# Moving one Relu and half of one scaling from ScalarE to VectorE in a sparse-attention and expert-routing kernel

## The chip, the core and the metric

The kernel runs on one core of a Trainium2 chip. The metric is the device time of one execution in microseconds (us). The engines are written as the profile writes them: PE is TensorE (matmuls), PEld its weight loads, ACT is ScalarE, DVE is VectorE, POOL is GpSimd and SP is SyncE. Each runs its own list of instructions in the order of the program and waits on semaphores that the other engines count up.

## The reference

Two layers stand behind each other. The first is an attention that selects chunks of 32 keys by an upper bound on their scores; the second sends each token to one of eight experts.

```python
def _attn_ref(q, k, v):                       # (4, 8, 768, 64) each
    k_min, k_max = min and max of k over each chunk of 32 keys
    ub = np.sum(np.maximum(q * k_min, q * k_max), axis=-1)     # a bound per query and chunk
    top_chunks = np.argsort(where(causal, ub, -1e9))[..., -6:]
    scores = where(selected and causal, q @ k.T / 8, -1e9)
    return softmax(scores) @ v

def _moe_ref(x, w_gate, w1, w2):              # x: (3072, 512), 8 experts, hidden size 1024
    expert_idx = np.argmax(x @ w_gate, axis=1); gate_w = its softmax probability
    for e in range(8):
        ye = np.maximum(x[expert_idx == e] @ w1[e], 0.0) @ w2[e]
        out[expert_idx == e] = gate_w[...] * ye
```

## The kernel before, in words

**Attention.** The 32 pairs of batch and head are worked off two heads at a time, in 16 steps called pairs (0 to 15). For a pair, `kt` and `qt` turn k and q on PE into PSUM tiles `pk` and `pq` (two banks each, from a pool of three buffers). From `pk`, DVE makes the maximum of each chunk (`kr0`) and its negated minimum (`kr1`) into the tile `KK`, and ACT makes a bfloat16 copy (`kc`). From `pq`, ACT makes three things: the positive part of q (`qR`), the positive part of -q (`qN`) and a bfloat16 copy (`qc`). The bound of the reference is then two products that PE adds up in the PSUM tile `pc` (`ub`): positive part of q with the maxima, positive part of -q with the negated minima. From `pc`, DVE finds the sixth-best chunk of each query (`sel1`, `selb`, `sel2a`, `sel2b`, `sel3`, `selt`) and makes the mask tile `mt`, which PE adds to the scores (`sc0` to `sc5`). ACT takes exponentials (`ex`), POOL cuts the causal diagonal (`cm`), PE multiplies with v (`av`), DVE adds up denominators (`ac`).

**Experts.** The tokens' rows are scattered to memory in expert order, and 26 tiles of 128 rows (j = 0 to 25) are read back. For each tile PE makes the hidden layer (`U`), ACT its Relu (`Rl`), a transposing DMA turns it (`H`), PE multiplies with w2 into the PSUM tile `py` of one bank (`D`), ACT scales the 512 columns by the row's gate weight into `y` (`Y`, the function `down_act`), and POOL issues an indirect DMA that writes the rows of `y` to the output (`O`). After the last tile every engine loads a count `late_i` and branches over a block for rare extra tiles.

**Order.** The order of the work is a list written out by hand, `ORDER`: each word is a step and its pair or tile, and each step issues its instructions on its engines at that place in the list. A tile framework adds the semaphore waits. Steps `z.n` are n matmuls on a zeroed tile without a use for the result, which fill TensorE's idle time at the start. ACT's list begins with the load of its function table; the framework puts it ahead of the first activation.

The change touches `qe` (which makes `qR` and `qN`), `down_act`, and one line of `ORDER`.

Of the kernel before, what the change touches and what calls it, by code (L numbers as in the profile page):

```python
# [9 lines left out]
FP32 = mybir.dt.float32  # L10
BF16 = mybir.dt.bfloat16
I32 = mybir.dt.int32
AF = mybir.ActivationFunctionType
ALU = mybir.AluOpType
# [8 lines left out]
def kernel(  # L23
# [10 lines left out]
    nc = tc.nc  # L34

    B, H, S, D = q.shape
# [5 lines left out]
    DM = H * D  # L42
# [12 lines left out]
    NS = NA + NL + ND + NF2  # L55
# [4 lines left out]
    Q0 = S - NQB * 64  # L60
# [162 lines left out]
    def qe(i, nm):  # L223
        s = st[i]
        s[nm] = work.tile([128, NQB, 2, 32], FP32, tag=nm, name=nm)
        nc.scalar.activation(s[nm][:].rearrange("p j c w -> p (j c w)"), s["pq"][:, Q0:S], AF.Relu,  # L226
                             scale=1.0 if nm == "qR" else -1.0)

    def qc(i):
        nc.scalar.activation(KQ[i % 2][:, 1], st[i]["pq"], AF.Copy)  # L230
# [287 lines left out]
    tag_all = const.tile([128, JT, 2], I32)  # L518
# [167 lines left out]
    fs = [dict() for _ in range(NTILE)]  # L686
# [3 lines left out]
    def kind(j):  # L690
        if j < NA + NL:
            return "whole", j
        if j < NA + NL + ND:
            return "mixed", NFULL + NF2 + j - NA - NL
        if j < NS:
            return "first", NFULL + j - NA - NL - ND
        if j < NS + NB - NL:
            return "whole", NA + NL + j - NS
        return "second", NFULL + NF2 + ND + j - NS - NB + NL
# [113 lines left out]
    def down_act(j):  # L813
        tag, pool, bufs = (("v", ld, LDB["v"]), ("ot", work, 2))[j % 2]
        y = pool.tile([128, DM], FP32, tag=tag, bufs=bufs, name="y")
        nc.scalar.activation(y[:], fs[j]["py"][:], AF.Copy, bias=0.0, scale=tag_all[:, kind(j)[1], 0:1].bitcast(FP32))  # L816
        fs[j]["y"] = y

    def put(j):
# [25 lines left out]
    def sm_c(i):  # L845
# [3 lines left out]
    rb_ = lambda f, *a: (lambda i: f(i // HP, *a))  # L849
    fn = dict(lk=sg(load, "k"), lq=sg(load, "q"), lv=sg(load, "v"), w=load_w,  # L850
              kt=kt, kr0=sg(kred, 0), kr1=sg(kred, 1), kc=kc, qt=qt, qR=sg(qe, "qR"), qN=sg(qe, "qN"), qc=qc, ub=ub_c,
              sel1=sel1, selb=selb, sel2a=sg(sel2, 0, 5), sel2b=sg(sel2, 5, NQB), sel3=sel3, selt=selt,
              ocB=sg(oc, 0), ocA=sg(oc, 1), sm=sm_c, gt=gt, uc=uc, ut=ut, rcp=rcp, lgt=lgt, lga=lga, xt=xt, xr=xr,
              ra=rb_(r_add), rb=rb_(r_max), rc=rb_(r_shift), rx=rb_(r_exp), rd=rb_(r_cand), re=rb_(r_first),
              rf=rb_(r_hot), rg=rb_(r_sum), rh=rb_(r_eps), ri=rb_(r_gate), rk=rb_(r_rank), rm=rb_(r_row),
              rn=rb_(r_pick), ro=rb_(r_slot), rp=rb_(r_int),
              g=gather, x=x_in, z=idle_mm, xc=x_tag, U=up_mm, Rl=up_act, H=up_turn, D=down_mm, Y=down_act, O=put, dr=lambda n: nc.gpsimd.drain(), sp=pause, wg=load_gate)
    for u in range(6):
        fn.update({f"sc{u}": sg(sc, u), f"ex{u}": sg(ex, u), f"cm{u}": sg(cm, u), f"av{u}": sg(av, u),
                   f"ac{u}": sg(ac, u), f"s{u}": rb_(r_scat, u)})  # L860

    def steps(gen, n, last):
# [7 lines left out]
    x_slots += [t_[:].rearrange("p a s -> p (a s)")[:, ds(512 * n, 512)] for t_ in (KQ[0], KQ[1]) for n in range(3)]  # L870

    ORDER = """
        lk.0 lq.0 lq.1 lk.1 lv.0 lv.1 wg.0 kt.0 z.2 qt.0 kr0.0 qN.0 qR.0 kr1.0 z.3 ub.0 kc.0 qc.0 qt.1 sel1.0 selb.0
        sel2b.0 kt.1 qR.1 sel2a.0 sel3.0 kc.1 qN.1 selt.0 qc.1 z.4 sc0.0 ex0.0 sc3.0 sc1.0 kr0.1 kr1.1 ex3.0 ex1.0
        ub.1 sel1.1 selb.1 sc2.0 ex2.0 cm3.0 lk.2 lq.2 w.19 sc4.0 av1.0 sel2b.1 sel2a.1 av2.0 kt.2 w.15 sc5.0 sel3.1
        ac2.0 selt.1 ex4.0 qt.2 qc.2 ex5.0 av3.0 qN.2 lq.3 kr0.2 cm4.0 kr1.2 ac4.0 cm0.0 ac3.0 cm5.0 av4.0 qR.2
# [71 lines left out]
    for step in ORDER.split():  # L948
        nm, n = step.split(".")
# [6 lines left out]
    with tc.If(more[0] > 0) as _:  # L956
        for j0 in range(NS, NTILE, 3):
            for j in range(j0, min(j0 + 3, NTILE)):
                gather(j)
                x_in(j)  # L960
                x_tag(j)
            for j in range(j0, min(j0 + 3, NTILE)):
                up_mm(j)
                up_act(j)
                up_turn(j)
            for j in range(j0, min(j0 + 3, NTILE)):
                down_mm(j)
                down_act(j)
                put(j)
# [35 lines left out]
```

## Time and profile before

| | |
|---|---|
| median of 3 runs | 302.18 us (299.79 to 308.25) |
| the profiled execution: its time | 299.35 us |
| its span, from the first to the last instruction | 297.5 us |
| outside the span | 1.85 us |
| PE busy | 285.5 us (96% of the span) |
| DVE busy | 197.2 us (66%) |
| ACT busy | 189.1 us (64%) |
| POOL busy | 156.9 us (53%) |

The start of the span (0 to about 13 us) is filled by loads and by the first pair's chain, the stretch up to about 202 us by attention, then up to 291.85 us by expert tiles; the last tile's output leaves after that. The time of an execution is the span and some 1.85 us around it. All rows below are of this one execution.

### The profile page before, as it was taken

How to read it: one execution, taken by the hardware profiler on the slowest of the kernel's cores; microseconds unless marked ns; L12 is line 12 of the kernel's file. 1: busy time of each engine (PE TensorE's matmuls, PEld its weight loads, DVE VectorE, ACT ScalarE, POOL GpSimd, SP SyncE). 2: the span in 40 equal slices, each digit the busy share in tenths (PEclk: the TensorE clock that was granted, in tenths of full speed). 3: DMA queues.
4: the chain of work that ended last, by engine and by line, in shares of the span. 5: the costliest groups of instructions: out<-in, count | busy, mean ns of one | idle time of the engine just before them, and what ended most of it. 6: DMA issues, size and time to landing. Idle time of an engine off the chain costs nothing.

```text
span 297.5 us, 8589 instructions
## 1 busy us (share of the span) xinstructions
PE 285.5 (96%) x3105; PEld 145.5 (49%) x3105; DVE 197.2 (66%) x613; ACT 189.1 (64%) x266; POOL 156.9 (53%) x245
## 2 busy tenths in 40 slices
PE   7899999998999999999999999999999999999992
PEld 3454554554555545555556555444444444444450
DVE  6687988989999999999999999885810312000000
ACT  1879778677777786777787877543443644444541
POOL 5064442652434657724468987431685557753543
PEclk9999999999999999999999999999999999999999
DMA  8999999898997999989999999899999999999662
GB/s 153 198 196 202 190 197 216 162 222 183 176 199 132 204 195 224 203 166 189 197 229 193 210 210 258 144 150 137 191 177 255 176 223 240 223 186 220 155 140 78
DMA packets 132587, 56.51 MB, mean 190 GB/s; under 512 B 121915, under 2 KB 121917, under 8 KB 132544
## 3 DMA queue, kind: packets, MB, share of 16 engines
q1 hardware_dynamic: 117440, 29.13, 53.9%
q0 software_dynamic: 12224, 26.78, 45.2%
q10 hardware_dynamic: 2880, 0.02, 1.7%
q8 instruction: 28, 0.46, 0.7%
q14 instruction: 15, 0.12, 0.1%
HBM read 53.26 MB, written 9.99 MB: 213 GB/s over the span
## 4 chain that ended last, share of the span: by engine, by line
PE 69%; DVE 12%; POOL 5%; issue 4%; DMA 4%; ACT 3%; SPq 1%; POOLq 0%; DVEq 0%; ACTq 0%
PE ph L783 15%; PE oa L324 14%; PE py L809 12%; DVE Pa L335 6%; PE ps L288 5%; PE pc L242 5%; PE ps L296 4%; PE pc L352 3%; DMA w_all<-in_moe_w_dram 2%; PE ob L324 2%; DVE KK L214 2%; PE pc L362 2%; PE px L199 2%; PE pq L208 2%; POOL out_dram L820 2%
## 5 line engine op out<-in xcount | busy, mean ns | idle before, releaser
L304 ACT ACTIVATE Pa<-ps 128x1024 f32<-128x1024 f32 x64 | 65.1, 1024 | 16.0 <-PE ps L296 12.6
L335 DVE TENSOR_TENSOR Pa<-Pa 128x1024 f32<-128x1024 f32 (+2 forms) x64 | 65.7, 1027 | 6.2 <-PE oa L324 1.9
L324 PE MATMUL oa<-Pa,v 128*64 128x512 f32 (+2 forms) x320 | 64.3, 518 | 0.0
L311 POOL TENSOR_SCALAR_AFFINE_SELECT Pa<-Pa 128x256 f32<-128x256 f32 x48 | 25.5, 547 | 52.0 <-ACT Pa L304 49.4
L809 PE MATMUL py<-w_all,hT 128*128 (+2 forms) x256 | 47.2, 379 | 0.0
L792 ACT ACTIVATE h<-ph 128x1024 bf16<-128x1024 f32 (+1 forms) x27 | 26.6, 991 | 26.7 <-DMA hT<-h 12.5
L288 PE MATMUL ps<-KQ 64*128 64x512 bf16 (+3 forms) x256 | 37.3, 307 | 1.1 <-ACT Pa L304 0.6
L820 POOL DMA_INDIRECT out_dram<-y,tag_all x26 | 25.6, 986 | 19.4 <-ACT y L816 14.9
L296 PE MATMUL ps<-mt,IND 64*128 64x256 bf16 (+4 forms) x512 | 34.2, 225 | 0.3 <-DVE mt L272 0.3
L500 POOL DMA_INDIRECT xs_dram<-xrow,sli x24 | 26.9, 1121 | 14.3 <-DVE cnt L527 5.6
L809 PEld LDWEIGHTS <-hT 128*128 128x128 bf16 (+1 forms) x256 | 20.8, 102 | 24.5 <-issue 1.7
L816 ACT ACTIVATE y<-py,tag_all 128x512 f32<-128x512 f32 x26 | 17.7, 686 | 21.1 <-PE py L809 17.5
L214 DVE TENSOR_REDUCE KK<-pk 128x24 f32<-128x768 f32 x32 | 29.1, 943 | 1.3 <-PE pk L208 1.3
L324 PEld LDWEIGHTS oa<-Pa,v 128*64 128x64 f32 x320 | 19.4, 136 | 19.8 <-issue 14.6
L288 PEld LDWEIGHTS <-KQ 64*128 64x128 bf16 x256 | 13.1, 93 | 28.4 <-issue 28.1
L296 PEld LDWEIGHTS <-IND 64*128 64x128 bf16 x512 | 23.1, 94 | 7.5 <-issue 0.4
L783 PE MATMUL ph<-w_all,x_early 128*128 (+1 forms) x128 | 25.5, 379 | 0.1
L182 POOL DMA_DIRECT2D w_all<-in_moe_w_dram x32 | 23.9, 747 | 0.0
L311 POOL TENSOR_SCALAR_AFFINE_SELECT Pb<-Pb 128x256 f32<-128x256 f32 x32 | 18.8, 614 | 9.5 <-ACT Pb L304 9.4
L783 PE MATMUL ph<-w_all,KQ 128*128 (+2 forms) x128 | 21.9, 380 | 0.0
L752 DVE TENSOR_TENSOR tag_all<-tag_all,inv_i 128x1 int32<-128x1 int32 x10 | 1.6, 162 | 28.0 <-DMA tag_all<-xs_dram 28.0
L226 ACT ACTIVATE qN<-pq 128x576 f32<-128x576 f32 x16 | 10.5, 653 | 14.8 <-PE pq L208 14.7
(167 smaller groups left out, 449.5 us busy)
## 6 DMA issues: line engine op xcount, KB each, us to landing
w_all<-in_moe_w_dram POOLq DMA_DIRECT2D x32, 512.0 KB, 6.6
k<-in_k_dram SPq DMA_DIRECT2D x32, 192.0 KB
q<-in_q_dram SPq DMA_DIRECT2D x32, 192.0 KB
v<-in_v_dram SPq DMA_DIRECT2D x32, 192.0 KB
hT<-h SPq DMA_TRANSPOSE x27
out_dram<-y,tag_all POOLq DMA_INDIRECT x26, 4.1
xs_dram<-xrow,sli POOLq DMA_INDIRECT x24, 6.5
tag_all<-xs_dram ACTq DMA_DIRECT2D x20, 1.0 KB
```

Source lines behind the costliest of these rows:

```text
L214: nc.vector.tensor_reduce(KK[i % 2][:, n, 0:NCH], st[i]["pk"].rearrange("p (c w) -> p c w", w=CH), AX.X, ALU.max if n == 0 else ALU.min, n ...
L288: nc.tensor.matmul(ps[:, hd, ds(c0, w)], lhsT=kc_[r, ts(kb_, 128)], rhs=qc_[r, ds(q0, w)], start=True, stop=False, skip_group_check=True)
L296: nc.tensor.matmul(o[:, :, c, :], lhsT=IND[c][r, ts(kb_, 128)], rhs=mt[r, ds(j0, n), :], start=False, stop=True, skip_group_check=True)
L304: nc.scalar.activation(P[:], st[i][f"ps{u}"][:, :, 0:w], AF.Exp)
L311: nc.gpsimd.affine_select(out=pd, in_=pd, pattern=[[0, 2], [1, 128]], compare_op=ALU.is_ge, fill=0.0, base=0, channel_multiplier=-1)
L324: nc.tensor.matmul(po[64 * hd:64 * hd + 64, ds(q0 - o0, w)], lhsT=vt[:, kb_, hd, :], rhs=P[:, hd, ds(c0, w)], start=(u <= 1 and n == 0), s ...
L335: nc.vector.tensor_tensor(a[:, :, ds(q0_, w)], a[:, :, ds(q0_, w)], P[:, :, ds(c0, w)], ALU.add)
L500: d = nc.gpsimd.indirect_dma_start(out=xs_dram[:], out_offset=bass.IndirectOffsetOnAxis(ap=sli[:, u:u + 1], axis=0), in_=bst[b]["xrow"][:, ...
L783: nc.tensor.matmul(ph[r, fh, :], lhsT=fs[j]["xT"][:, c, r], rhs=w1_all[:, ds(wo + c * F + fh * 512, 512)], start=(c == 0), stop=(c == NDC ...
L792: nc.scalar.activation(h_[:, a].rearrange("q a (c j p) -> q (a c) j p", c=2, j=2), fs[j]["ph"][:, a].rearrange("q a (c p j) -> q (a c) j p ...
L809: nc.tensor.matmul(py[r], lhsT=fs[j]["hT"][:, c, r], rhs=w2_all[:, ds(wo + c * DM, DM)], start=(c == 0), stop=(c == NFC - 1), skip_group_c ...
L820: d = nc.gpsimd.indirect_dma_start(out=out[:], out_offset=bass.IndirectOffsetOnAxis(ap=tag_all[:, kind(j)[1], 1:2], axis=0), in_=fs[j]["y" ...
```

## The change: what it does

For pair 0 alone, the positive part of -q (`qN.0`) is made by DVE, as a multiplication by -1 and a maximum with 0, in place of an ACT Relu with scale -1. In `ORDER` the step is moved from ahead of `qR.0` to behind `kr1.0`. For the last expert tile alone (j = 25), ACT scales columns 0 to 255 of `py` and DVE columns 256 to 511.

```diff
     def qe(i, nm):
         s = st[i]
         s[nm] = work.tile([128, NQB, 2, 32], FP32, tag=nm, name=nm)
-        nc.scalar.activation(s[nm][:].rearrange("p j c w -> p (j c w)"), s["pq"][:, Q0:S], AF.Relu,
-                             scale=1.0 if nm == "qR" else -1.0)
+        dst = s[nm][:].rearrange("p j c w -> p (j c w)")
+        if (i, nm) == (0, "qN"):
+            nc.vector.tensor_scalar(dst, s["pq"][:, Q0:S], -1.0, 0.0, ALU.mult, ALU.max)
+        else:
+            nc.scalar.activation(dst, s["pq"][:, Q0:S], AF.Relu, scale=1.0 if nm == "qR" else -1.0)
...
     def down_act(j):
...
-        nc.scalar.activation(y[:], fs[j]["py"][:], AF.Copy, bias=0.0, scale=tag_all[:, kind(j)[1], 0:1].bitcast(FP32))
+        gate, w = tag_all[:, kind(j)[1], 0:1].bitcast(FP32), DM // 2 if j == NS - 1 else DM
+        nc.scalar.activation(y[:, 0:w], fs[j]["py"][:, 0:w], AF.Copy, bias=0.0, scale=gate)
+        if w < DM:
+            nc.vector.tensor_scalar(y[:, w:DM], fs[j]["py"][:, w:DM], gate, None, ALU.mult)
...
     ORDER = """
-        lk.0 lq.0 lq.1 lk.1 lv.0 lv.1 wg.0 kt.0 z.2 qt.0 kr0.0 qN.0 qR.0 kr1.0 z.3 ub.0 kc.0 qc.0 qt.1 sel1.0 selb.0
+        lk.0 lq.0 lq.1 lk.1 lv.0 lv.1 wg.0 kt.0 z.2 qt.0 kr0.0 qR.0 kr1.0 qN.0 z.3 ub.0 kc.0 qc.0 qt.1 sel1.0 selb.0
```

Three places of the instruction lists follow, with the semaphores that each instruction waits for: `PE_49` counts PE's instructions, `DVE_49` VectorE's, `Activation_49` ScalarE's, `Pool_49` GpSimd's, and names with DMA count transfers. Lines behind 226 have numbers higher by 3 in the changed kernel, behind 816 by 6.

ScalarE's list from its first instruction, before:

```order
L226 ACT_TABLE_LOAD
L226 ACTIVATE qN<-pq 128x576 [waits PE_49]
L226 ACTIVATE qR<-pq 128x576 [waits DVE_49,Pool_49]
L218 ACTIVATE KQ_124<-pk 128x768 [waits DVE_49]
L230 ACTIVATE KQ_124<-pq 128x768
L226 ACTIVATE qR<-pq 128x576 [waits PE_49,Activation_49]
```

ScalarE's list at the same place now:

```order
L230 ACT_TABLE_LOAD [waits DVE_49,PE_49]
L230 ACTIVATE qR<-pq 128x576 [waits Pool_49]
L218 ACTIVATE KQ_124<-pk 128x768 [waits DVE_49]
L233 ACTIVATE KQ_124<-pq 128x768 [waits DVE_49]
L230 ACTIVATE qR<-pq 128x576 [waits PE_49,Activation_49]
```

The first activation is now `qR.0`, which has three waits, and two of them (VectorE, and PE for the last transpose of `qt.0`) stand ahead of the table load instead of behind it; the copy `qc.0` (L233) has a new wait for VectorE.

VectorE's list around the chunk reductions of pair 0, before:

```order
L167 TENSOR_SCALAR tri_164<-rev_150 128x8 x8
L214 TENSOR_REDUCE KK_126<-pk 128x24 [waits PE_49]
L214 TENSOR_REDUCE KK_126<-pk 128x24
L251 STREAM_TRANSPOSE ubm<-pc 128x288 [waits PE_49]
L255 TENSOR_TENSOR ubm<-ubm,cbp 128x9 [waits DVE_49]
```

VectorE's list at the same place now:

```order
L167 TENSOR_SCALAR tri_164<-rev_150 128x8 x8
L214 TENSOR_REDUCE KK_126<-pk 128x24 [waits PE_49]
L214 TENSOR_REDUCE KK_126<-pk 128x24
L228 TENSOR_SCALAR qN<-pq 128x576 [waits Activation_49]
L254 STREAM_TRANSPOSE ubm<-pc 128x288 [waits PE_49]
```

`qN.0` comes third behind the two reductions and waits for ScalarE's first activation, `qR.0`, which reads the same PSUM tile `pq`.

VectorE's list where the straight-line program ends (`tag_all` holds the gate weights and token numbers), before:

```order
L755 TENSOR_TENSOR tag_all<-xg_4447,inv_i 128x1 [waits DMASW2_49]
L756 COPY tag_all<-xg_4447 128x1
L755 TENSOR_TENSOR tag_all<-xg_4447,inv_i 128x1 [waits DMASW4_49]
L756 COPY tag_all<-xg_4447 128x1
L953 TENSOR_LOAD late_i [waits DVE_49]
L956 COMPARE_AND_BRANCH
```

VectorE's list at the same place now:

```order
L758 TENSOR_TENSOR tag_all<-xg_4447,inv_i 128x1 [waits DMASW4_49]
L759 COPY tag_all<-xg_4447 128x1
L822 TENSOR_SCALAR y<-py,tag_all 128x256 [waits DMASW5_49,DMASW7_49,DMASW3_49,Activation_49]
L959 TENSOR_LOAD late_i [waits DVE_49]
L962 COMPARE_AND_BRANCH
```

VectorE's half of the last `y` waits for ScalarE's half of it, and the last output DMA on POOL, which waited for `Activation_49` before, now waits for `DVE_49`.

## Rows read from the trace of the kernel before

**Rows 1.** The table of busy time by stretch, attention and expert stages
```profile
core 0: us, PE busy (x) PEld busy (x) DVE busy (x) ACT busy (x) POOL busy (x), PEclk, DMA share, GB/s
24.00:60.00 36.00, 35.56 (x492) 18.86 (x490) 31.59 (x84) 28.16 (x41) 16.08 (x28) 1.00 1.04 193
60.00:100.00 40.00, 39.05 (x544) 21.04 (x540) 37.25 (x115) 30.34 (x46) 16.07 (x30) 1.00 0.99 185
202.00:282.00 80.00, 79.87 (x434) 36.41 (x436) 17.33 (x98) 37.38 (x46) 45.53 (x57) 1.00 1.08 198
```

**Rows 2.** Waits of PE, 12 to 202 us: total, times, longest
```profile
PE pk L208 <- DVE xrow L422: 0.9, 1, 0.9
PE ps L288 <- ACT Pa L304: 0.6, 1, 0.6
PE ps L288 <- ACT KQ L230: 0.4, 1, 0.4
```

**Rows 3.** The timeline of ACT, 0 to 11 us: start, duration
```profile
0.81 1.28 ACT L226 ACT_TABLE_LOAD   x1 [0.81 <-PEq L989]
7.78 0.65 ACT L226 ACTIVATE qN<-pq 128x576 f32<-128x576 f32 x1 [5.68 <-PE pq L208]
8.32 0.65 ACT L226 ACTIVATE qR<-pq 128x576 f32<-128x576 f32 x1
8.86 0.82 ACT L218 ACTIVATE KQ<-pk 128x768 bf16<-128x768 f32 x1
9.55 0.83 ACT L230 ACTIVATE KQ<-pq 128x768 bf16<-128x768 f32 x1
10.86 0.65 ACT L226 ACTIVATE qR<-pq 128x576 f32<-128x576 f32 x1 [0.49 <-PE pq L208]
```

**Rows 4.** The timeline of PE, 1 to 11 us
```profile
1.26 3.60 PE L109 MATMUL pz<-wz 128*128 128x512 bf16 x8 [1.26 <-DVE wz L107]
5.15 0.90 PE L208 MATMUL pk<-ident,k 64*128 64x64 f32 x12 [0.29 <-DMA k<-in_k_dram]
...
7.15 0.59 PE L208 MATMUL pq<-ident,q 64*128 64x64 f32 x12 [0.21 <-DMA q<-in_q_dram]
7.67 0.82 PE L109 MATMUL pz<-wz 128*128 128x512 bf16 x3
9.07 0.69 PE L242 MATMUL pc<-qR,KK 64*32 64x288 f32 x8 [0.57 <-issue]
9.55 0.69 PE L242 MATMUL pc<-qN,KK 64*32 64x288 f32 x8
10.17 0.59 PE L208 MATMUL pq<-ident,q 64*128 64x64 f32 x12
```

**Rows 5.** The timeline of DVE, 5.9 to 11 us
```profile
6.09 1.82 DVE L214 TENSOR_REDUCE KK<-pk 128x24 f32<-128x768 f32 x2 [1.26 <-PE pk L208]
10.30 0.48 DVE L251 STREAM_TRANSPOSE ubm<-pc 128x288 f32<-128x288 f32 x1 [2.39 <-PE pc L242]
```

**Rows 6.** Groups of DVE by form: busy us, mean ns, idle before
```profile
L214 DVE TENSOR_REDUCE KK<-pk 128x24 f32<-128x768 f32 x32 | 29.1, 943 | 1.3 <-PE pk L208 1.3
L251 DVE STREAM_TRANSPOSE ubm<-pc 128x288 f32<-128x288 f32 x16 | 7.6, 476 | 4.7 <-PE pc L242 4.5
L122 DVE TENSOR_SCALAR IND<-colc,pm 128x768 bf16<-128x768 bf16 x2 | 1.1, 568 | 0.4 <-POOL colc L114 0.4
```

**Rows 7.** Waits of ACT, 24 to 202 us
```profile
ACT KQ L218 <- DVE KK L214: 6.6, 9, 1.8
```

**Rows 8.** The timeline at the end, 291 us to the end of the span
```profile
290.82 1.03 PE L809 MATMUL py<-w_all,hT 128*64 128x512 bf16 x8
...
291.94 0.69 ACT L816 ACTIVATE y<-py,tag_all 128x512 f32<-128x512 f32 x1 [1.04 <-PE py L809]
292.91 0.97 POOL L820 DMA_INDIRECT out_dram<-y,tag_all  x1 [0.76 <-ACTq L956]
```

**Rows 9.** Groups of ACT by form: busy us, mean ns, idle before
```profile
L816 ACT ACTIVATE y<-py,tag_all 128x512 f32<-128x512 f32 x26 | 17.7, 686 | 21.1 <-PE py L809 17.5 <-issue 2.2 <-PE ph L783 1.1
L343 ACT ACTIVATE ot<-oa 128x512 f32<-128x512 f32 x16 | 9.6, 603 | 0.7 <-PE oa L324 0.7
L341 ACT ACTIVATE ot<-ob 128x256 f32<-128x256 f32 x16 | 6.4, 398 | 0.0
```

**Rows 10.** Issue to landing of the output DMAs, 280 us on
```profile
DMA to landing us min/median/max: 2.5/2.6/2.8
```

## Prediction, written before the result

> **What bounds the kernel now.** Read the table of stretches first, for the engine that is busy without a break [rows 1]. PE works 35.56 of 36 us, 39.05 of 40 and, in the expert stage, 79.87 of 80. The waits of PE say whether what little is left hangs on a fixed clock [rows 2]: the longest from 12 to 202 us are 0.9, 0.6 and 0.4 us, all of them on DVE or ACT, which work in the same chain, and none on a transfer. So PE's fixed list is the bound from about 12 us to 291.85, and there is no pause on a transfer in which a later start could be made up: what the first 12 us gain or lose moves everything behind it, and what follows the last matmul is added at the end. The change sits in exactly these two places, so each is read as a chain by its timeline.
>
> The head [rows 3 to 5]: `qt.0` ends on PE at 7.15 + 0.59 = 7.74. ACT starts `qN.0` at 7.78 and `qR.0` at 8.32 (ends 8.97), then the copies `kc.0` at 8.86 and `qc.0` at 9.55. PE's products with `qR` start at 9.07 (PE's spare matmuls had ended at 8.49, so PE stands still for 0.58 us), those with `qN` at 9.55; DVE takes over their result at 10.30, and ACT's next activation follows PE's `qt.1` at 10.86. DVE has its two reductions behind it at 6.09 + 1.82 = 7.91 and is then idle for 2.39 us: this is the idle time that the change wants to use.
>
> The tail [rows 8, 10]: the last matmul ends at 291.85, ACT scales from 291.94 to 292.63, POOL's output DMA starts 0.28 later, at 292.91, and its data land 2.6 us or so behind that.
>
> **The change part by part: the head.** The intended gain is plain: if DVE made `qN.0` from 7.91 on while ACT made `qR.0` from 7.78 to 8.43, PE could start about half a us earlier than 9.07. Two waits in the instruction lists speak against it.
>
> First, ACT's table load. It takes 1.28 us and ran at 0.81, while ACT had nothing to do until 7.78 [rows 3]. In the changed list the load stands behind a wait for PE's `qt.0`, and so cannot start before about 7.78, where `qN.0` started; it ends at 9.06. `qR.0` takes 0.65: 9.06 to 9.71, which is 0.74 later than the 8.97 of before.
>
> Second, DVE's `qN.0` waits for `qR.0`. Before, ACT also waited for DVE in front of its copy of `pk`, nine times in the attention stage, 6.6 us in all [rows 7]: readers of one PSUM tile on two engines go one after the other in this program. So `qN.0` starts at about 9.75 (DVE began its reductions 0.04 behind the end of the instruction that it waited for, 5.15 + 0.90 = 6.05 to 6.09 [rows 4, 5]). No row shows a DVE tensor-scalar operation on fp32 in PSUM. The nearest rows are a reduction of 768 columns from PSUM, 0.943 us, and a transpose of 288 columns from PSUM, 0.476 [rows 6]: (0.943 - 0.476) / 480 = 0.97 ns per column, so 576 columns come to 0.476 + 288 x 0.00097 = 0.76. The lower end is the only wide tensor-scalar row, 768 bf16 columns from SBUF in 0.568; the upper end is the whole reduction, 0.943. I take 0.76, because both of its rows read fp32 from PSUM. It ends at 10.51; PE started 0.07 to 0.10 behind the end of `qR.0` before (8.97 to 9.04-9.07), so the `qN` products start at 10.51 + 0.08 = 10.59 instead of 9.55: **+1.04 us**. The `qR` products fit in between (9.79 to 10.48).
>
> Who stands behind that wait? On PE the whole list: `qt.1`, `kt.1` and the scores. On ACT, `kc.0` can run at 9.60 to 10.42 (it starts 0.54 behind `qR.0`, as 8.32 to 8.86), but `qc.0` reads `pq` too and now waits for DVE: 10.55 instead of 9.55, +1.00; then `qR.1` waits for `qt.1`, +1.04 as PE. On DVE, the selection of pair 0 waits for PE's products: 10.30 + 1.04. All three chains move alike, so nothing behind them is free of it. The ACT work that is saved, 0.54 us between the starts of two activations, gives nothing back here, since ACT is the one that waits. The bounds: with 0.568 for DVE +0.85, with 0.943 +1.22. At 10.86 ACT had waited 0.49 us for `qt.1`; that pause is no cushion, as `qt.1` itself comes later. SP's and POOL's queues are not passed by the step: it issues no DMA.
>
> **The tail.** ACT's half: 512 columns without a gate operand take 0.603, 256 columns 0.398, so 256 columns are worth 0.205, and half of the 0.686 operation comes to 0.48 [rows 9]: 291.94 to 292.42. DVE's half waits for it (both read the one bank of `py`) and starts at 292.46. By the two PSUM rows above 256 columns are 0.476 - 32 x 0.00097 = 0.44, no less than half of 0.568 = 0.28 and no more than the transpose's 0.48 [rows 6]. It ends at 292.90 in place of 292.63, and POOL's DMA starts 0.28 behind: **+0.27 us** (+0.11 to +0.31). A gain is excluded here as long as the wait stands. The other three waits of DVE's half are for output DMAs of tile 21 and earlier ones, four and more tiles back; ACT waits for the last of them before as well. DVE's branch behind it is not on the path: POOL waits for the landing until after 295.
>
> **The sum.** 1.04 + 0.27 = +1.31 us, bounds 0.96 to 1.53. Against the profiled execution: 299.35 + 1.31 = 300.66. That execution is one of the fast ones: the timed runs are 299.79, 302.18 and 308.25. The middle of these three and the profiled one is (299.79 + 302.18) / 2 = 300.99, and I set the change on that: **302.3 us**. From the median, 302.18, it would be 303.5.
>
> **The rivals.** (1) The change does what it is meant to: both engines read at the same time, the load is early. Then the `qR` products start at 8.53 in place of 9.07 (-0.5) and the last `y` is ready at about 292.42 (-0.2): 299.35 - 0.7 = 298.6, and from 300.99, 300.3. For it: DVE is idle at both places [rows 5, 8]. Against it: the waits in the lists, and [rows 7]. By the Trainium skill, "PSUM — Partial Sum Buffer", section "PSUM bank collisions raise a hardware error", two engines must not read one bank in the same partitions at the same time, even different columns; by that rule this rival could not even be had by taking the waits away, and the sum stays as it is.
>
> (2) The load is done early after all, as in the row of before, and only the two readers go one after the other. Then `qR.0` is 7.78 to 8.43, `qN.0` 8.47 to 9.23, the `qN` products start at 9.31 (-0.24), and with the tail's +0.27 the change is worth nothing: 299.4, from the middle run 301.0. For it: the load's place in time before was not tied to its activation. Against it: the wait stands ahead of the load in ACT's list.
>
> (3) The load costs more than its row shows. Between its end at 2.09 and the next activation ACT was idle 5.68 us [rows 3], so anything that follows a load was covered; now it would lie on the path, with a price between 0 and 5.68. I take 0 for the forecast, because the row ends at 1.28 and ACT shows no further work. A price near the load's own length would bring +2.6 in all, 302.0, from the middle run 303.6. By the Trainium skill, "ScalarE: Activation LUTs", section "What ACT_TABLE_LOAD costs", a load takes about 1283 ns and a drain of about 1380 ns comes with each switch to another set; by that the sum would be 1.31 + 1.38 = +2.69, and no run here shows the drain.
>
> (4) Slower: PE falls back to 1.2 GHz. PE stood still 0.58 us ahead of the `qR` products; now it is 8.49 to 9.79, 1.30 us, and another 0.1 ahead of the `qN` products. The longest pause with a row is 0.9, at a granted clock of 1.00 [rows 1, 2]. At the start PE did run at the lower level: eight spare matmuls took 3.60, 0.45 each, three later ones 0.82, 0.27 each, and twelve transposes 0.90 at 5.15 against 0.59 at 7.15 [rows 4]. It took from 1.26 to about 7, some 5.9 us, until the higher level showed. If the longer pause cost the level and it came back as slowly, about half of 5.9 us would be added: +2.9, 299.35 + 1.31 + 2.9 = 303.6, from the middle run 305.2. It decides once a pause of 1.3 us is enough; the spare matmuls right ahead of it speak against that.
>
> **How the numbers follow.** Forecast 0.72; rival 1 0.04; rival 2 0.10; rival 3 0.09; rival 4 0.05. The low end, 299.7, lies between the forecast's least sum on the fastest execution (299.35 + 0.96 = 300.3) and rival 2 there (299.4). The high end, 305.0, is rival 3 on the median run (302.18 + 2.7 = 304.9). A measurement of this kernel tells about 2%, 6 us, from no change: the three runs alone spread by 8.5. No case reaches 6 us by its mechanism; an unlucky median may. So faster 0.01, same 0.96, slower 0.03.
>
> **What the profile will show.** Right, if the table load stands at about 7.8 instead of 0.81; if DVE's `qN` starts behind the end of ACT's `qR` and takes about 0.76; if PE's `qN` products start near 10.6 and the scores of pair 0 about 1 us later than before; and if at the end DVE's half starts behind ACT's and the last DMA starts some 1.3 us later than 292.91. Wrong, if the load stands early, if more than 0.1 us lies between the load's end and `qR.0`, if a later wait of PE shrinks by the same amount, or if the matmuls around 10 us take twice as long.

## The result, and the profile after

The changed kernel took 303.05 us (median of 20 runs, 301.03 to 311.41), the kernel before, timed beside it, 301.66 us (20 runs, 299.58 to 309.32). The ratio is 1.0061, 95% interval [1.0040, 1.0082]: slower by 1.2 to 2.5 us, which is within 2%. All ratios here leave disturbed executions out (those over 1.5% above the fastest of their kernel), so they are not ratios of the medians beside them. Timed again, beside a kernel before of 305.38 us, the ratio was 1.0063 [1.0026, 1.0101]. The forecast was 302.3 us, and with a chance of 0.96 a change of less than 2%.

The profiled execution of the changed kernel took 303.97 us; its span is 302.1.

PE's timeline at the start (start, duration, idle before and its releaser) answers to [rows 4]:

```profile
7.28 0.59 PE L208 MATMUL pq<-ident,q 64*128 64x64 f32 x12 [0.95 <-DMA q<-in_q_dram]
7.80 0.82 PE L109 MATMUL pz<-wz 128*128 128x512 bf16 x3
9.98 0.69 PE L245 MATMUL pc<-qR,KK 64*32 64x288 f32 x8 [1.36 <-issue]
10.73 0.69 PE L245 MATMUL pc<-qN,KK 64*32 64x288 f32 x8
11.35 0.59 PE L208 MATMUL pq<-ident,q 64*128 64x64 f32 x12
```

ACT's timeline of the same stretch answers to [rows 3]:

```profile
7.94 1.28 ACT L230 ACT_TABLE_LOAD   x1 [7.94 <-PE pq L208]
9.23 0.65 ACT L230 ACTIVATE qR<-pq 128x576 f32<-128x576 f32 x1
9.78 0.81 ACT L218 ACTIVATE KQ<-pk 128x768 bf16<-128x768 f32 x1
10.71 0.81 ACT L233 ACTIVATE KQ<-pq 128x768 bf16<-128x768 f32 x1
12.04 0.65 ACT L230 ACTIVATE qR<-pq 128x576 f32<-128x576 f32 x1 [0.52 <-PE pq L208]
```

DVE's timeline answers to [rows 5]:

```profile
9.92 0.76 DVE L228 TENSOR_SCALAR qN<-pq 128x576 f32<-128x576 f32 x1 [2.27 <-ACT qR L230]
11.49 0.48 DVE L254 STREAM_TRANSPOSE ubm<-pc 128x288 f32<-128x288 f32 x1 [0.81 <-PE pc L245]
```

Read the three together from `qt.0`, which ends at 7.28 + 0.59 = 7.87. ACT's function table is loaded only then, at 7.94 instead of 0.81. `qR.0` follows 0.01 us behind the load, DVE's `qN.0` 0.04 behind the end of `qR.0`, PE's products with `qN` 0.05 behind the end of that. They start 2.86 us behind `qt.0`, where they started 1.81 behind it before (9.55 - 7.74, [rows 4]): +1.05. From here on, distances are counted from the end of `qt.0`, since transfers and PE's clock make it end at 7.62 to 8.41 in one execution or another.

The timeline of the end answers to [rows 8]:

```profile
296.26 0.47 ACT L820 ACTIVATE y<-py,tag_all 128x256 f32<-128x256 f32 x1 [1.04 <-PE py L812]
296.77 0.48 DVE L822 TENSOR_SCALAR y<-py,tag_all 128x256 f32<-128x256 f32 x1 [22.71 <-ACT y L820]
297.53 0.97 POOL L826 DMA_INDIRECT out_dram<-y,tag_all  x1 [1.06 <-DVE y L822]
```

The two halves stand one behind the other; from ACT's start to the last DMA it is 1.27 us, 0.97 before [rows 8]: +0.30.

What lies between is seen in the table of busy time by stretch, for [rows 1], and in the waits of PE from 13 to 290 us, for [rows 2] (total, times, longest):

```profile
24.00:60.00 36.00, 35.56 (x498) 18.96 (x498) 31.59 (x82) 27.90 (x42) 16.08 (x28) 1.00 1.02 192
60.00:100.00 40.00, 38.89 (x552) 21.00 (x544) 36.92 (x109) 30.19 (x46) 15.80 (x29) 1.00 1.02 183
202.00:282.00 80.00, 78.37 (x446) 35.93 (x444) 18.72 (x104) 35.28 (x44) 42.08 (x52) 1.00 1.11 194
```

```profile
PE ph L786 <- issue: 1.7, 2, 1.4
PE pk L208 <- DMA k<-in_k_dram: 1.3, 2, 0.9
PE pk L208 <- DVE xrow L425: 1.1, 1, 1.1
```

From 24 to 60 us PE works the same 35.56 us as before; what the head lost stays lost. The last DMA starts 297.53 - 292.91 = 4.62 us later than in the profiled execution before. To place that, I took each pair's transpose of the bounds (`ubm` on DVE) and each Relu of the expert stage, and its start in the one trace less its start in the other:

| near us | 16 to 60 | 72 to 96 | 108 | 180 | 198 | 284 | last DMA |
|---|---|---|---|---|---|---|---|
| later by, us | 1.18 | 1.32 | 2.25 | 2.41 | 2.77 | 4.32 | 4.62 |

1.18 is the head (+1.05, and `qt.0` itself ended 0.13 later), the last 0.30 the tail. The 3.1 between them are not the change's as far as the experiments tell, but for 0.15 (below): two executions of the kernel before, alike within 0.1 us up to 96 us, differ by 8 to 11 us behind 155.

### The profile page after: what moved, and what is told of

The parts are those of the page before. It is cut to its first block, busy times and chain, and to the rows that moved or that the text cites. A ratio compares the mean times of both kernels' runs of the same rounds, so it can differ in the third digit from the quotient of the medians.

```text
span 302.1 us, 8592 instructions
## 1 busy us (share of the span) xinstructions
PE 285.3 (94%) x3105; PEld 145.3 (48%) x3105; DVE 198.1 (66%) x615; ACT 188.2 (62%) x265; POOL 158.2 (52%) x245
## 4 chain that ended last, share of the span: by engine, by line
PE 69%; DVE 12%; DMA 7%; ACT 4%; issue 3%; POOL 2%; SPq 1%; POOLq 0%; DVEq 0%; ACTq 0%
PE ph L786 14%; PE oa L327 14%; PE py L812 13%; DVE Pa L338 6%; PE ps L291 5%; PE pc L245 4%; PE ps L299 4%; PE pc L355 4%; DMA k<-in_k_dram 3%; DMA x_early<-xs_dram 3%; PE pc L365 2%; PE ob L327 2%; DVE KK L214 2%; PE px L199 2%; PE pq L208 2%
## 5 line engine op out<-in xcount | busy, mean ns | idle before, releaser
L820 ACT ACTIVATE y<-py,tag_all 128x512 f32<-128x512 f32 (+1 forms) x26 | 17.3, 677 | 17.0 <-PE py L812 12.7
L314 POOL TENSOR_SCALAR_AFFINE_SELECT Pb<-Pb 128x256 f32<-128x256 f32 x32 | 20.8, 676 | 10.1 <-ACT Pb L307 9.6
L786 PEld LDWEIGHTS <-x_early 128*128 128x128 bf16 (+1 forms) x128 | 11.1, 101 | 15.1 <-DMA x_early<-xs_dram 1.7
```

The costliest lines, as they stand in the source:

```text
L314: nc.gpsimd.affine_select(out=pd, in_=pd, pattern=[[0, 2], [1, 128]], compare_op=ALU.is_ge, fill=0.0, base=0, channel_multiplier=-1)
L786: nc.tensor.matmul(ph[r, fh, :], lhsT=fs[j]["xT"][:, c, r], rhs=w1_all[:, ds(wo + c * F + fh * 512, 512)], start=(c == 0), stop=(c == NDC ...
```

## The experiments

Each run has the kernel before timed on the same chip; the chips are not all equally fast (before: 305.06, 305.95, 305.38 and 302.30 us in four groups of runs). Most of the traces (one of each run) show waits of PE on transfers or on ACT behind 100 us, so they are read at the two places, and the times only beside them.

| run | products with qN behind `qt.0`, us | ACT's last start to last DMA | time, us | ratio to before |
|---|---|---|---|---|
| before (profile) | 1.81 | 0.97 | | |
| after (profile) | 2.86 | 1.27 | 303.05 | 1.0061 [1.0040, 1.0082] |
| head_only | 3.05, at the lower clock | 0.96 | 308.41 | 1.0092 [1.0053, 1.0132] |
| tail_only | 2.00, at the lower clock | see text | 306.51 | 0.9994 [0.9954, 1.0034] |
| early_load | 1.59 | 1.27 | 307.85 | 1.0105 [1.0041, 1.0170] |
| late_load | 2.61 | 0.96 | 305.86 | 1.0051 [1.0015, 1.0087] |
| early_qr_first | 1.33 | 0.96 | 307.22 | 1.0007 [0.9959, 1.0054] |
| after_again | 2.87 | 1.27 | 306.85 | 1.0063 [1.0026, 1.0101] |
| early_load_2 | 1.59 | 1.27 | 308.13 | none, see text |
| early_qr_first_2 | 2.27, at the lower clock | 0.96 | 305.99 | 0.9977 [0.9934, 1.0019] |
| early_load_head | 1.96, at the lower clock | 0.96 | 302.96 | 1.0035 [0.9990, 1.0081] |

**One part of the change alone.** head_only keeps `qN.0` on DVE and its place in the order, and has the old `down_act`:

```diff
-        if w < DM:
-            nc.vector.tensor_scalar(y[:, w:DM], fs[j]["py"][:, w:DM], gate, None, ALU.mult)
```

> Only pair 0's qN moves to VectorE; the last tile is scaled as before. Two distances are compared, since they are read to 0.05 us: head, from the end of qt.0's transposes to the start of the qN products on PE (1.81 us before, 2.86 changed), and tail, from the end of the last matmul to the last output DMA (1.06 before, 1.36 changed). My theory (the late table load and the reader that waits): head 2.86, tail 1.06, the time about 1.05 us or 0.35% over the kernel before. Rival: the measured +0.6% is more than my sum of 1.31 because the head's delay grows in the attention stage; then the steps of pairs 1 to 15 lag by more and more, and the time is 0.5% or more over.

The load stands at 8.48, right behind `qt.0`, and the products with `qR` 2.12 behind it, as in the changed kernel. Those with `qN` came out at 3.05 instead of 2.86, because PE ran at the lower of its two levels there (three spare matmuls took 1.46 us in place of 0.82, eight products 1.19 in place of 0.69). That began ahead of the place of the change; it is taken up below. The tail is that of the kernel before, 0.96.

Its time is a miss: 0.53 to 1.32% over the kernel before, where 0.35% were expected and the rival set 0.5% or more. The rival's growing delay is not in the trace: `ubm` is 2.78 us later than before at pair 1 and 2.94 at pair 8, and the 0.15 between them fall at one place (below). What the clock shows beyond the head is not explained.

tail_only has the old `qe` and `ORDER` and the new `down_act`.

> Only the last tile is shared between the engines. My theory: head 1.81, tail 1.36 (ScalarE 0.47, then VectorE 0.48, one behind the other), the time 0.3 us or 0.1% over the kernel before, which the timing can hardly tell from nothing. Rival: the halves cost nothing or gain, and the whole change's loss is the head's; then tail is 1.06 or less.

Its time cannot be told from before, as expected of +0.3 us, but its end does not answer the question: the 1.36 expected cannot be read off. Its head is 2.00 for 1.81, with PE at the lower clock. The timeline of the end:

```profile
296.94 0.60 PE L809 MATMUL py<-w_all,hT 128*64 128x512 bf16 x4
298.18 1.05 ACT L817 ACTIVATE y<-py,tag_all 128x512 f32<-128x512 f32 x2 [3.44 <-PE py L809]
299.14 0.97 POOL L823 DMA_INDIRECT out_dram<-y,tag_all  x1 [2.03 <-ACT y L817]
299.26 0.48 DVE L819 TENSOR_SCALAR y<-py,tag_all 128x256 f32<-128x256 f32 x1 [22.86 <-ACTq L959]
300.42 0.97 POOL L823 DMA_INDIRECT out_dram<-y,tag_all  x1 [0.31 <-DVEq L959]
```

ACT was late: it ran the last two scalings (x2) only at 298.18, behind a pause of 3.44 us, so POOL was still busy with the DMA of tile 24 until 300.11, and DVE's half had been ready at 299.74. That DVE's half stands behind ACT's holds here too; why ACT paused is not shown.

**The load alone.** late_load is the kernel before with one word of `ORDER` moved, so that `qR.0`, with its several waits, is the first activation. DVE has no part in it.

```diff
-        ... qt.0 kr0.0 qN.0 qR.0 kr1.0 z.3 ub.0
+        ... qt.0 kr0.0 qR.0 qN.0 kr1.0 z.3 ub.0
```

> The kernel before, with qR.0 ahead of qN.0 in the order, both on ScalarE: nothing is moved to VectorE, but the first activation is the one with three waits, so that the load stands behind qt.0. My theory: load at qt.0's end + 0.07, then qR, then qN 0.54 behind: head 0.07 + 1.28 + 0.54 + 0.65 + 0.08 = 2.62, the time 0.8 us or 0.27% over the kernel before. Rival: a load costs more than its row, with a drain near 1.4 us behind it: head 4.0, time +2.2 us. Second rival: the load is harmless: head 1.81.

ACT's timeline of it:

```profile
7.94 1.28 ACT L226 ACT_TABLE_LOAD   x1 [7.94 <-PE pq L208]
9.24 0.65 ACT L226 ACTIVATE qR<-pq 128x576 f32<-128x576 f32 x1
9.79 0.64 ACT L226 ACTIVATE qN<-pq 128x576 f32<-128x576 f32 x1
```

The table load moves to `qt.0` by this alone. `qN` products at 2.61, expected 2.62; `ubm` of the pairs up to 100 us is 1.02 us later than before, and the time is longer by 0.15 to 0.87%.

**The load early.** early_load is the changed kernel with an activation of one column at the start, of the zeroed tile of the spare matmuls, whose result nobody reads. The load can then go first:

```diff
     idle_mm(8)
+    warm = const.tile([128, 1], FP32, name="warm")
+    nc.scalar.activation(warm[:], spare["w"][:, 0:1], AF.Relu)
```

> The whole change, and one tiny ScalarE activation of a zeroed column right at the start, so that the table load comes first and its wait is not qt.0's. My theory: the load runs near 1 us; head falls from 2.86 to 0.04 + 0.65 + 0.04 + 0.76 + 0.08 = 1.57, which is 0.24 less than before the change; the tail stays 1.36; the time is that of the kernel before (+0.06 us). Rival: VectorE's wait and its operation are the cost, not the load: head stays near 2.9 and the time near +1.3 us.

early_qr_first has the same activation and the order of late_load, and so differs from early_load's head only in that ACT makes `qN.0`.

> The kernel before with the tiny activation at the start (early table load) and qR.0 ahead of qN.0, both on ScalarE: PE's first products need qR first. My theory: the qR products start 0.77 us behind qt.0's end, the qN products at 0.04 + 0.54 + 0.65 + 0.08 = 1.31 (1.81 before); pair 1's transposes follow, held by ScalarE's copy of pk, which stays where it was, so that the head gives 0.4 to 0.5 us and the time -0.4 us or -0.13%. Rival: pair 1's k or q lands no earlier than it was used before, and the gain ends there: the selection of pair 1 starts as before and the time is unchanged.

In both the load stands at 0.81 and `qR.0` starts right behind `qt.0`. The timelines of early_load, ACT and then DVE:

```profile
0.81 1.28 ACT L113 ACT_TABLE_LOAD   x1 [0.81 <-PEq L997]
2.11 0.20 ACT L113 ACTIVATE warm<-wz 128x1 f32<-128x1 bf16 x1
8.00 0.65 ACT L232 ACTIVATE qR<-pq 128x576 f32<-128x576 f32 x1 [5.69 <-PE pq L210]
```

```profile
8.68 0.76 DVE L230 TENSOR_SCALAR qN<-pq 128x576 f32<-128x576 f32 x1 [0.86 <-ACT qR L232]
10.25 0.48 DVE L256 STREAM_TRANSPOSE ubm<-pc 128x288 f32<-128x288 f32 x1 [0.81 <-PE pc L247]
```

PE's timeline of early_qr_first, and one line of early_load's:

```profile
7.09 0.60 PE L210 MATMUL pq<-ident,q 64*128 64x64 f32 x12
9.02 0.69 PE L244 MATMUL pc<-qN,KK 64*32 64x288 f32 x8
10.63 0.59 PE L210 MATMUL pk<-ident,k 64*128 64x64 f32 x12 [0.32 <-DMA k<-in_k_dram]
```

```profile
10.93 0.58 PE L210 MATMUL pk<-ident,k 64*128 64x64 f32 x12 [0.23 <-DMA k<-in_k_dram]
```

In early_load DVE is free from 7.81 on and still starts at 8.68, 0.03 behind ACT. So the four versions add up: 1.33 us with the load early and both parts on ACT; + 1.28 with the load late = 2.61 (late_load, measured 2.61); + 0.25 or so with `qN` on DVE (1.59 against 1.33) = 2.86 (the changed kernel, measured 2.86). DVE as the second reader costs 0.25 us more than ACT, because ACT's second activation starts 0.55 behind its first, ahead of that one's end, and DVE's only behind it and takes 0.76.

early_qr_first makes 0.48 us of gain at this place, of which 0.15 are left from pair 1 on: PE then waits 0.32 us for the first `k` of pair 1, as the run's rival had it. early_load loses 0.2 of its 0.22 us in the same way, by a wait of 0.23. On the clock early_qr_first is not told from before (1.0007 and 0.9977).

early_load's time did not come out. Its trace up to 100 us is near the theory (`ubm` at the start 0.05 us earlier than before, then 0.14 and from pair 6 on 0.29 later, with `qt.0` 0.17 later), yet it was timed at 1.0105, from six runs. So it was timed again, together with the changed kernel and early_qr_first.

> The changed kernel with the load early, timed again, since its first timing (1.0105) stood against its trace (head 0.24 us earlier than before, tail 0.30 later). The theory expects a ratio of 1.000 to the kernel before, inside its interval, and the first timing to have been scatter of few runs; the rival that the early activation costs some 2 to 3 us somewhere behind the start expects 1.008 to 1.010 again.

> The changed kernel once more, beside the two kernels below on one chip. The theory (a late table load and two readers in turn at the start, two readers in turn at the end) expects its products with qN 2.86 us behind the end of the first qt, the last output DMA 1.27 us behind the start of ACT's last scaling, and a ratio to the kernel before of 1.004 (+1.3 us). The rival that something else than these two places costs the time expects a ratio over 1.008.

> The kernel before with the load early and qR ahead of qN on ACT, the best head of the versions tried: products with qN 1.33 us behind qt, 0.5 earlier than before. The theory expects a ratio of 0.998 to 1.000 to the kernel before, and below that of the changed kernel by some 1.5 us; the rival that an early activation costs some us somewhere expects over 1.005.

early_load's second timing settles nothing. Its median again lay 2.8 us above before (308.13 to 305.38), but its six runs spread from 303.18 to 313.25, those of before from 302.23 to 314.04, and the two that a ratio would count average 304.62 us, those of before 304.61. Its head and tail read as the first time (1.59 and 1.27), with `ubm` within 0.1 us of the profiled execution before from pair 1 to 108 us. early_load_head then kept its head and took the old tail.

> The head of early_load (qN by VectorE, the table load early) with the tail of the kernel before. Its place is to find where early_load loses the 2.8 us that its head and tail don't show. The theory of the two places expects products with qN 1.57 us behind qt, 0.24 earlier than before, the last DMA 0.97 behind ACT's last start, and a ratio to the kernel before of 0.999. The rival that VectorE's part at the start with an early load costs something further on expects 1.008 to 1.010 here too. If it comes out at 0.999, the loss lies in the two places together or is scatter.

1.0035 [0.9990, 1.0081] reaches from the one answer, 0.999, to the other, 1.008. In its one trace the expert stage is 1.1 us later than in the trace of before, of which 0.44 stand at pair 0, where PE was again at the lower level. Whether early_load loses anything is therefore open: its first timing alone says so. The early activation by itself costs nothing that the clock tells (early_qr_first has it too), and nothing in the traces ahead of 100 us shows a loss of that size.

**Two engines at a time.** bank_split puts `qt.0` into two tiles of different banks, so that ACT and DVE can work on the two halves crosswise, with the load early:

```diff
-        ... qt.0 kr0.0 qN.0 qR.0 kr1.0 z.3 ub.0
+        ... qt.0 kr0.0 qRb.0 kr1.0 qNa.0 qRa.0 qNb.0 z.3 ub.0
```

> The intended overlap, made legal: pair 0's q is turned into two PSUM tiles of one bank each, ScalarE makes qR of the second bank while VectorE makes qN of the first, then they change places; the table load is early; the last tile is as before. My theory: readers of one bank take turns, readers of two banks need not: VectorE's first piece starts beside ScalarE's first, without waiting for it; the qR products start about 1.05 us behind qt.0's end, the qN products at about 1.54 (1.81 before), a gain of 0.27 us. Rival: reads of PSUM by two engines slow each other even in two banks: 384 columns take clearly more than 0.49 on ScalarE or 0.57 on VectorE.

ACT and DVE of it, by their timelines:

```profile
7.71 0.49 ACT L246 ACTIVATE qR<-pqb 128x384 f32<-128x384 f32 x1 [5.40 <-PE pqb L209]
8.10 0.32 ACT L246 ACTIVATE qR<-pqa 128x192 f32<-128x192 f32 x1
```

```profile
7.69 0.35 DVE L244 TENSOR_SCALAR qN<-pqa 128x192 f32<-128x192 f32 x1
8.23 0.56 DVE L244 TENSOR_SCALAR qN<-pqb 128x384 f32<-128x384 f32 x1 [0.19 <-ACT qR L246]
```

Here they do start together, at 7.69 and 7.71, as the change meant it. The `qN` products came 1.43 behind `qt.0`, 0.38 earlier than before and 0.10 later than early_qr_first: `qR` in two pieces is ready 0.80 us behind `qt.0` (8.10 + 0.32 - 7.62), in one piece 0.73 in early_qr_first, and PE then needs 0.49 for the products with `qR`, in which either engine would have `qN` ready. So even the reading side by side that rival 1 speaks of gains nothing over a mere exchange of order on ACT. Within one bank they still take turns: DVE's second piece waits for ACT's first. By the Trainium skill, "PSUM — Partial Sum Buffer", section "PSUM bank collisions raise a hardware error", two engines may read different banks at the same time. The trace agrees, and shows no slowing: ACT's 192 and 384 columns took 0.32 and 0.49 with DVE reading beside it for more than half of each, its 576 columns 0.65 with DVE idle (8.32 in [rows 3]), steps of 0.17 and 0.16. The one execution of this kernel, 311.86 us with a wait of 3.0 us for a transfer of `q`, says nothing on its time.

tail_free takes away what makes the last halves wait: DVE scales the last 256 columns of tile 24's product instead of tile 25's, so those columns of the last tile's rows are not the reference's.

```diff
-            nc.vector.tensor_scalar(y[:, w:DM], fs[j]["py"][:, w:DM], gate, None, ALU.mult)
+            nc.vector.tensor_scalar(y[:, w:DM], fs[j - 1]["py"][:, w:DM], gate, None, ALU.mult)
```

> The whole change, but VectorE's half of the last tile's output is taken from the tile before it (columns 256 to 511 of tile 25's output are tile 24's product, so that part is left out); VectorE then reads another bank and need not wait for ScalarE's half. My theory: tail is 0.09 + 0.47 + 0.28 = 0.84, 0.22 less than before the change, which is what two halves at the same time would have given; head 2.86. Rival: the output DMA, with two engines to wait for, starts no earlier: tail 1.06 or more.

The timeline of its end:

```profile
295.13 0.48 DVE L822 TENSOR_SCALAR y<-py,tag_all 128x256 f32<-128x256 f32 x1 [20.77 <-ACT y L820]
...
296.84 0.47 ACT L820 ACTIVATE y<-py,tag_all 128x256 f32<-128x256 f32 x1 [1.83 <-PE py L812]
297.58 0.97 POOL L826 DMA_INDIRECT out_dram<-y,tag_all  x1 [0.66 <-issue]
```

From ACT's start to the last DMA it is 0.74 us, 0.47 and 0.27, against 1.27 with the wait and 0.97 before. The expected 0.84 was counted from the last matmul, and that came to 1.21, since ACT started 0.47 behind it in place of 0.09. The same late start (0.43 to 0.45) shows in early_load and in after_again, each time behind a scaling of an earlier tile that ACT had run late; why is open. Its time is of one execution too (304.08 us).

**The kernel before, once more.**

> The kernel before, unchanged, profiled a second time, to see how far two executions of one list differ in the middle. My theory: head 1.81 and tail 1.06 within 0.05 us, while waits of PE for transfers of k and q come and go: in the changed kernel's profile PE waited 1.3 us for k, in the first profile of the kernel before for none, so here anything from 0 to 3 us, at other places. Rival: no such waits here either; then the 1.3 us belong to the change.

It took 310.32 us. Head and tail are 1.82 and 1.05, as expected; `ubm` of pair 0, at 10.23, is within 0.1 us of the first trace, and the expert stage is 10 to 11 us behind it. Its waits of PE from 13 to 290 us, to be held against [rows 2]:

```profile
PE pk L208 <- DMA k<-in_k_dram: 5.5, 2, 5.1
PE ps L288 <- ACT Pa L304: 1.4, 1, 1.4
PE pc L199 <- issue: 1.0, 1, 1.0
```

The same list of instructions waits 5.1 us for one transfer here and for none in the first trace. So the later part of one trace says little on a change of 1 us.

## Why the prediction was right

The time was right, 303.05 us for 302.3, and so were both mechanisms. Of the 0.75 us between the two times 0.67 are the base: the kernel before came out at 301.66, where the forecast had set 300.99 from four executions.

- **The load on the path.** Forecast to start right behind `qt.0` and to be followed by `qR.0` without a gap: 7.94, and 0.01 us of gap. What stands behind it came as forecast, allowing for `qt.0` 0.13 later: `kc.0` 9.78 for 9.60, `qc.0` 10.71 for 10.55. late_load shows that the order of the two activations does this alone, early_load and early_qr_first that a trifling activation ahead of it takes the load back to 0.81. Rival 2 (load early) and rival 3 (a price beyond the row) fall for the changed kernel. By the Trainium skill, "ScalarE: Activation LUTs", section "What ACT_TABLE_LOAD costs", a drain of about 1380 ns comes with each switch to a different set of tables; none is seen at this first load, whose next activation starts 0.01 us behind it.
- **Readers in turn.** DVE starts 0.04 behind ACT at both places (0.03 in early_load), and in bank_split, with two banks, beside it. Rival 1 fails on this, as forecast.
- **DVE's price.** 0.76 us for 576 columns was estimated from a reduction and a transpose, and 0.76 was measured; the wide operation on bf16 would have been the wrong neighbour. For 256 columns 0.44 was estimated and 0.48 measured, with ACT's half 0.47 for 0.48.
- **The sum.** Head +1.05 for +1.04, tail +0.30 for +0.27. 1.35 us are 0.45% of 301.66, inside the interval of 0.40 to 0.82% at its lower end.
- **What the clock does not show.** The changed kernel's two ratios agree with the sum, but head_only (1.0092 [1.0053, 1.0132]) and the first timing of early_load (1.0105 [1.0041, 1.0170]) lie above what the two places give them, some 0.4 and 0.1%. The two mechanisms are shown by the distances in the traces; that they make up all of the 0.6% is not shown.
- **A term that was missed.** All seven traces (of five kernels) in which DVE makes `qN.0` in one instruction are another 0.15 us late from pair 6 on (1.17 to 1.32 in the changed kernel, 2.78 to 2.94 in head_only, 0.14 to 0.29 in early_load); in the traces without it, and in bank_split, where DVE makes it in two, the lag does not move at that place (0.02 us at most). PE's wait for DVE's `xrow` is 1.1 in place of 0.9 [rows 2]. DVE's timelines of the place, before and then in the changed kernel:

```profile
63.70 2.16 DVE L335 TENSOR_TENSOR Pa<-Pa 128x768 f32<-128x768 f32 x2 [0.28 <-PE oa L324]
65.96 0.92 DVE L335 TENSOR_TENSOR Pa<-Pa,Pc 128x512 f32<-128x512 f32 x1
```

```profile
64.87 1.63 DVE L338 TENSOR_TENSOR Pa<-Pa 128x768 f32<-128x768 f32 x1 [0.28 <-PE oa L327]
66.97 0.43 DVE L338 TENSOR_TENSOR Pa<-Pa 128x256 f32<-128x256 f32 x1 [0.46 <-DVE Pa L338]
67.50 0.70 DVE L338 TENSOR_TENSOR Pa<-Pa,Pc 128x512 f32<-128x512 f32 x1
```

  Before, the operation on 512 columns takes 0.92 us; in the changed kernel it takes 0.70, but comes 0.37 later behind the first `Pa` (2.63 for 2.26), by a pause of 0.46 that names no other engine: +0.37 - 0.22 = +0.15. DVE's list has one instruction more ahead of it here. In bank_split, with two more, the operation on 512 columns takes 0.92 again, so a mere count of instructions does not explain it; the cause is open. The prediction had all that follows the head move by the same amount, and here it does not: with this term the change costs 1.50 us, 0.50%.
- **Rival 4, PE's clock.** PE paused 1.36 us and its products kept 0.69 us per eight, in the changed kernel as in after_again: the longer pause did not cost the level. But the level does fall at this place in some executions. In early_qr_first_2 the windows say 1.00 of the clock until 7.8 us and 0.52 from there to 11.2; PE's timeline:

```profile
5.63 0.60 PE L109 MATMUL pz<-wz 128*128 128x512 bf16 x2
7.33 0.59 PE L210 MATMUL pq<-ident,q 64*128 64x64 f32 x12 [1.09 <-DMA q<-in_q_dram]
7.85 1.45 PE L109 MATMUL pz<-wz 128*128 128x512 bf16 x3
9.22 1.19 PE L244 MATMUL pc<-qR,KK 64*32 64x288 f32 x8
10.19 1.18 PE L244 MATMUL pc<-qN,KK 64*32 64x288 f32 x8
11.30 0.59 PE L210 MATMUL pq<-ident,q 64*128 64x64 f32 x12
```

  It went from 2.4 to 1.2 GHz behind a wait of 1.09 us for a transfer, ahead of the place of the change, and back at about 11.2; `ubm` came 3.52 us behind `qt.0` in place of 2.10 in early_qr_first, +1.4 us, where the prediction priced such a fall at 2.9. The changed kernel waited 0.95 there and after_again 1.13, and neither fell. What decides it is open.
- **What was said too broadly.** "None on a transfer" holds for the one execution of [rows 2]; in others PE waits up to 5.3 us on one. Two gains of the first 12 us were swallowed by such a wait, 0.33 us of early_qr_first and 0.2 of early_load; the changed kernel's loss was not. And a measurement tells smaller changes than the 2% named: with 20 executions of each kernel the interval was 0.21% to either side and left no change out.

## What to carry to other kernels

Before moving the first activation of a kernel, look at what it waits for: the function table's load stands with it, and 1.28 us that cost nothing at 0.81 us lay wholly on the path behind `qt.0`; an activation of one column at the start, of data that is there early, keeps the load out of the way in the traces, though no timing here shows the gain. Two engines that read one PSUM tile work in turn in this program, so moving half of a read to a second engine makes the chain longer by the second engine's whole operation less what the first would still have needed. An exchange of the order in which one engine makes two operands (early_qr_first, 0.48 us earlier at the place) was worth more than the help of a second engine, and still too little for the clock to tell.

## What the runs showed of the hardware

- Operations of DVE with a constant or a pointer on fp32 in PSUM: 192 columns 0.35 us, 256 with a pointer 0.48, 384 0.56, 576 0.76. Those of ACT: 192 0.32, 256 with a pointer 0.47, 384 0.49, 576 0.65, with the next one starting 0.10 to 0.11 before the end.
- In the first 12 us PE's clock takes another course from one execution to the next: in tail_only and early_load_head it was still at the lower level at 8 us (three spare matmuls 1.46 us), in head_only and early_qr_first_2 it fell back to it, in the others it was at the higher one from 5 to 7 us on. Counted from `qt.0` to `ubm`, this moved pair 0 by 0.2 us (tail_only) to 1.4 us (early_qr_first_2), as much as the change did.
